# An attention, mixture and gated-layer kernel: its opening written out as one list of single steps

## The chip, the cores and the metric

The kernel runs on one core of one Trainium2 chip. The metric is the device time of one execution in microseconds (us). Of the engines, TensorE (PE) multiplies, its weight load (PEld) runs beside it, VectorE (DVE), ScalarE (ACT) and GpSimd (POOL) do the elementwise work, and SyncE (SP) issues nearly all transfers. Each engine runs its own instructions in the order in which the program lists them.

## The reference

```
# q, k, v: (4, 8, 576, 64) f32; chunks of 64 along the sequence
scores = q_c @ k_c.T / sqrt(64);  attn = softmax(scores);  out = attn @ v_c
x = out laid out as (2304, 512)
p = domain_probs / (sum + 1e-9)
x1 = sum_e p[:, e] * (relu(x @ w1[e]) @ w2[e])        # 4 experts, 512 -> 1024 -> 512
y  = (silu(x1 @ w_gate) * (x1 @ w_val)) @ w_out        # 512 -> 1536 -> 512
```

## The kernel before, in words

Tokens go in 18 blocks of 128; a pass holds 6 blocks (two halves of 3), and there are three passes for each of the two layers. Products are made in float16 from a high and a low part of each operand (three products for one). A weight set n is a 512 x 256 part of w1, loaded as four quarters of 128 x 1024 numbers in all. From set 3 on, a set is multiplied by a seven-product scheme on sums and differences of quarters (`PRODUCTS`, `product`, tiles `lx`, `lz`, `lw`); sets 0 to 2 of the first pass are made plainly, as 12 plain products (`plain`, tiles `plx`, `ply`, `plz`, `plw`) of 12 matmuls of 128x384 each.

The first pass starts while the attention of its own six blocks is still being made. For a block a: `att_scores` (s), `att_max`, `att_sub`, `att_exp` (e), `att_parts` and `att_sums` (row sums, hs, sm, rs), `att_turn` and `att_turned` (transpose et), `att_values` (av), `att_scale`, `att_out` (transpose xt), then `out_high`, `out_copy` and `out_low`, which write the float16 high and low parts (b11, b21 for blocks 0 to 2; t4, b22 for blocks 3 to 5) and a float32 copy x0. `first_sums`, `first_sum4` and `first_split` make t1 to t4 from these copies.

Before float16 parts are made, values and weights are scaled by a power of two that comes from a norm. For the values v of each block and for each w1 set this norm is a sum of squares on ScalarE (`squares`, tile waste), summed over partitions by a one-column product with ones on TensorE (`total`). The scaling of w1 (`w1_scaled`, L548) and of w2 (`w2_scaled`, L837) is a multiply on GpSimd, for all 16 sets, in place, before the sums of quarters (L558, DVE), the high part (ACT, L137) and the low part (POOL, L138).

The order of the opening is a string of one-letter steps, `FIRST_BLOCKS`; after it come a few hand-placed groups (`next_plain`, `ahead`) up to the first seven-product step, and then a loop over products with work put off by `later` (a count of products) and `next_of_rest` (the attention of blocks 6 to 17). PSUM places are named A, X, Y (two buffers each), Z and W (one each). In the opening a load of q, k or v for a later block is issued where the place that it takes is read for the last time.

Of the kernel before, what the change touches and what calls it, by code (L numbers as in the profile page):

```python
# [95 lines left out]
def attention_moe_gated(  # L96
# [251 lines left out]
    def att_scores(a, where):  # L348
        s = att[a]
        ps = att_ps(f"s{a}", where)  # L350
        for i in range(NPAIR):
            for c in range(2):
                b = slice(64 * c, 64 * c + 64)
                nc.tensor.matmul(
                    ps[b, 2 * i : 2 * i + 2], s["q"][:, i, b], s["k"][:, :, i, c], start=True, stop=True
                )
        if next_in_place(a) is not None and a not in (4, 5):
            att_load(next_in_place(a))
        s["s"] = ps
        if a >= BLOCKS:  # L360
            att_max(a)
            att_sub(a)
# [43 lines left out]
    def att_parts(a):  # L406
        s = att[a]
        w = CH // 2
        whole = s["hs"] = by_pair(st_p.tile([P, H, w], F32, tag="hs", name=f"hs{a}", bufs=1))
        part = pairs(s["e"])  # L410
        nc.gpsimd.tensor_tensor(out=whole, in0=part[:, :, :, :w], in1=part[:, :, :, w:], op=ALU.add)
        part = whole[:, :, :, : w // 2]
        nc.gpsimd.tensor_tensor(out=part, in0=part, in1=whole[:, :, :, w // 2 :], op=ALU.add)

    def att_sums(a):
        s = att[a]
        sm = st_p.tile([P, H], F32, tag="sm", name=f"sm{a}")
        part = s["hs"][:, :, :, : CH // 4] if a < HALF else pairs(s["e"])
# [17 lines left out]
    def att_values(a, where):  # L436
        s = att[a]
        ps = att_ps(f"av{a}", where)
        for i in range(NPAIR):
            for c in range(2):  # L440

                nc.tensor.matmul(
                    ps[64 * c : 64 * c + 64, 2 * i : 2 * i + 2],
                    s["et"][:, 2 * i + c, :], s["v"][:, :, i, c], start=True, stop=True,
                )
        if next_in_place(a) is not None and a not in (4, 5):
            att_load_v(next_in_place(a))
        s["av"] = ps
        if a >= BLOCKS:
            att_scale(a)  # L450
# [42 lines left out]
    def out_low(a):  # L493
        for i, (h, l) in enumerate(out_ops(a)):
            r = slice(2 * i, 2 * i + 2)
            if a % HALF == HALF - 1:
# [6 lines left out]
    def first_sums(j):  # L503


        b1, b2 = x_first[0, j], x_first[1, j]
        d0, d1 = slice(0, 2), slice(2, 4)
        sub(b1[:, d0], b2[:, d0], b1[:, d0])
        sub(b2[:, d0], b2[:, d1], b2[:, d0])
        sub(b2[:, d1], b2[:, d1], b1[:, d0])  # L510

    def first_sum4(j):
        b1, b2 = x_first[0, j], x_first[1, j]
# [1 line left out]

    FIRST_PLACES = {"t1": (0, slice(0, 2)), "t3": (1, slice(0, 2)), "t2": (1, slice(2, 4)), "t4": (0, slice(2, 4))}

    def first_split(b, j):
        half, d = FIRST_PLACES[b]
        r = slice(j * P, (j + 1) * P)  # L520
        h, l = x_slots(0, b)
        split(h[:, :, r], l[:, :, r], x_first[half, j][:, d], nc.gpsimd if b in ("t3", "t4") else None)


    raw1, wop = {}, {}
# [598 lines left out]
    with tc.manual_schedule():  # L1124
# [51 lines left out]
        att_load(2)  # L1176
        nc.scalar.activation(junk, ident[:, :1], AF.Exp)
        att_load_v(1)
        att_load(3)
        att_load_v(2)  # L1180
# [11 lines left out]

        def plain_done():
            done(*made_plain.pop(0))

        def next_plain():
            plain_product(plain_banks[12 - len(pieces)])
            plain_done()

        def tick():  # L1200
            for f in deferred.pop(now[0], []):
# [17 lines left out]
        def own_col(n):  # L1219
            cols[n] = small(f"col_{n}", 1, BF16)  # L1220
            squares(raw1[n][:, 0:4].rearrange("p b f -> p (b f)"), cols[n], f"w1_{n}")

        def own_scale(n, place):
            w1_scale_of(n, total(cols[n], f"w1_{n}", places[place]))

        def own_col2():
            cols["w2"] = w2_col(0, BF16)

        def own_scale2(place):
            w2_scale_of(0, total(cols["w2"], "w2", places[place]))  # L1230

        cols = {}

# [9 lines left out]
        stages = {  # L1243
            "s": at(att_scores), "m": at(att_max), "d": at(att_sub), "x": at(att_exp), "p": at(att_parts),
            "r": at(att_sums), "t": at(att_turn), "c": at(att_turned), "v": at(att_values), "u": at(att_scale),
            "o": at(att_out), "h": at(out_high), "y": at(out_copy), "l": at(out_low),
            "f": lambda n: fetch_w1(n, False), "F": fetch_w1, "k": att_load_v, "L": att_load,
            "n": att_norm, "N": lambda a, b, place: att_norms(a, b, places[place]),
            "a": own_col, "b": own_scale, "A": lambda i: w2_greatest(0, i), "B": lambda i: own_col2(), "C": lambda place: own_scale2(place),
            "D": lambda i: w2_scaled(0, i), "S": w1_scaled,  # L1250
            "w": lambda i: w_plain(i // 2, HALVES[i % 2]),
            "P": lambda place: plain_product(place.lower()), "E": plain_done, "G": second_weights, "g": lambda j: split_w2(0, j), "q": lambda i: shares(),
        }
        FIRST_BLOCKS = (
# [4 lines left out]
        )  # L1259
        for step in FIRST_BLOCKS.split():  # L1260
            stages[step[0]](*(int(c) if c.isdigit() else c for c in step[1:]))
        del raw1[0], raw1[1], raw1[2]
        now[0] = -10
        fetch_w1(4)
        fetch_w1(5)
        next_plain()
        first_sums(0)
        tick()
        next_plain()
        first_sums(1)  # L1270
        split_w2(0, 2)
        tick()
        next_plain()
        first_sums(2)
        split_w2(0, 3)
        tick()
        next_plain()
        for j in range(HALF):
            first_split("t2", j)
        for _ in range(3):  # L1280
            tick()

        rest = []
        for a in range(BLOCKS, NS + 2):
# [44 lines left out]


        two = layer2(0)

        def ahead(*makes):

            if len(rest) % 2 == 0:
                next_plain()
            for _ in range(9):
                next(two)
            for make in makes:
                make()  # L1340
            next_of_rest()
            tick()

        def first_t3():
            for j in range(HALF):
                first_split("t3", j)

        def first_t1():
            for j in range(HALF):
                first_split("t1", j)  # L1350

        def first_sum4s():
            for j in range(HALF):
                first_sum4(j)

        ahead(first_t1, lambda: w_sums(raw1[3], None, 0), lambda: make_w(3, 0), lambda: fetch_w2(1, 0), lambda: fetch_w2(1, 1))
        ahead(first_sum4s, lambda: make_w(3, 2), lambda: fetch_w2(1, 2), lambda: fetch_w2(1, 3))
        ahead(lambda: w_sums(raw1[3], None, 1), first_t3, lambda: w2_scale_later(1, 1, 0))
        ahead(lambda: make_w(3, 4))
        for j in range(HALF):  # L1360
            later(1 + j, lambda j=j: first_split("t4", j))
        for j in range(4):
            later(4 + j, lambda j=j: split_w2(1, j))

# [171 lines left out]
```

## Time and profile before

| what | us |
|---|---|
| median of 3 runs (lowest, highest) | 1228.3 (1227.84, 1230.06) |
| the profiled execution, its span | 1228.85, 1227.0 |
| PE busy, share of the span | 1164.1 (95%) |
| DVE busy | 899.2 (73%) |
| ACT busy | 617.5 (50%) |
| POOL busy | 611.0 (50%) |

A share over the whole span hides stages with different limits: PE's clock row stands at full nearly everywhere except in the first tenth and around a quarter of the span. Durations of PE rows are modelled ends; how far apart the starts of consecutive rows are tells what a matmul costs in a stream.

### The profile page before, as it was taken

What the parts mean: (1) busy time and instruction counts of PE and PEld (TensorE: products, weight loads), DVE (VectorE), ACT (ScalarE), POOL (GpSimd) and SP (SyncE); (2) the same over time, 40 slices, a digit from 0 to 9 for tenths busy, and PEclk for the clock granted to TensorE, in tenths of its full rate; (3) what the DMA queues carried; (4) which work ended last, traced back from release to release, by engine and by line L of the source; (5) the groups of instructions that cost most, each with busy time, mean ns of one, the idle gap of its engine ahead of it and who ended that gap; (6) DMA issues with size and microseconds to landing.
All of it is one profiled execution on the core that took longest, in us unless ns stands there. A gap on an engine that the chain in (4) does not pass through costs nothing.

```text
span 1227.0 us, 20554 instructions
## 1 busy us (share of the span) xinstructions
PE 1164.1 (95%) x7287; PEld 693.4 (57%) x7287; DVE 899.2 (73%) x1738; ACT 617.5 (50%) x1263; POOL 611.0 (50%) x533
## 2 busy tenths in 40 slices
PE   6788999999889999999999999999999999999998
PEld 5445555555445545555555555555666666766766
DVE  6478667676556779897758988666488876787577
ACT  6545656564454445564645455435544444444442
POOL 4338665779874467774637776601143222222121
PEclk9789999999899999999999999999999999999999
DMA  7327456556686464757567765573565554455433
GB/s 240 106 86 244 150 191 206 187 161 203 201 301 187 153 213 171 244 182 265 169 203 246 247 214 193 165 239 103 126 233 180 180 184 152 155 188 189 144 117 104
DMA packets 157528, 227.57 MB, mean 185 GB/s; under 512 B 15201, under 2 KB 77281, under 8 KB 157425
## 3 DMA queue, kind: packets, MB, share of 16 engines
q1 hardware_dynamic: 156496, 224.78, 56.8%
q10 hardware_dynamic: 896, 1.44, 0.4%
q8 instruction: 57, 0.93, 0.3%
q14 instruction: 47, 0.38, 0.1%
q0 software_dynamic: 32, 0.04, 0.0%
HBM read 166.17 MB, written 60.03 MB: 184 GB/s over the span
## 4 chain that ended last, share of the span: by engine, by line
PE 55%; DVE 6%; DMA 4%; POOL 2%; issue 2%; ACT 2%; SPq 1%; POOLq 0%; DVEq 0%; ACTq 0%
PE lx L955 6%; PE lx L956 6%; PE lx L957 6%; PE y L1006 6%; PE y L1008 6%; PE y L1004 6%; PE ox L1073 4%; PE oz L1073 4%; PE lz L955 3%; PE lz L957 3%; PE lz L956 3%; DMA w<-w 2%; PE lw L955 1%; PE lw L956 1%; PE lw L957 1%
## 5 line engine op out<-in xcount | busy, mean ns | idle before, releaser
L1006 PE MATMUL y<-w,hh 128*128 128x512 f16 x576 | 220.0, 382 | 7.6 <-POOL w L138 7.6
L1004 PE MATMUL y<-w,hh 128*128 128x512 f16 x576 | 220.1, 382 | 3.7 <-ACT hh L879 2.0
L138 POOL TENSOR_TENSOR ol<-sg,oh 128x384 f16<-128x384 f32 x72 | 75.1, 1052 | 295.1 <-ACT oh L137 253.2
L1008 PE MATMUL y<-w,hl 128*128 128x512 f16 x576 | 219.9, 382 | 0.8 <-DVE hl L882 0.8
L955 PEld LDWEIGHTS <-w 128*128 128x128 f16 x1182 | 116.5, 99 | 83.6 <-issue 5.5
L956 PEld LDWEIGHTS <-w 128*128 128x128 f16 x1182 | 116.4, 98 | 83.2 <-issue 9.7
L957 PEld LDWEIGHTS <-w 128*128 128x128 f16 x1182 | 116.4, 99 | 82.5 <-issue 7.1
L138 POOL TENSOR_TENSOR w<-raw,w 128x512 f16<-128x512 f32 (+1 forms) x96 | 107.7, 1134 | 78.3 <-ACT w L137 52.0
L879 ACT ACTIVATE hh<-sum_p 128x384 f16<-128x384 f32 x90 | 46.8, 520 | 196.1 <-DVE sum_p L943 195.7
L1102 DVE SCALAR_TENSOR_TENSOR acc<-y,pg,acc 128x512 f32<-128x512 f32 x126 | 92.0, 744 | 67.3 <-PE y L1008 65.3
L1008 PEld LDWEIGHTS <-hl 128*128 128x128 f16 x576 | 56.6, 98 | 79.0 <-issue 10.3
L943 DVE TENSOR_TENSOR sum_p<-lx,p 128x384 f32<-128x384 f32 x81 | 44.8, 553 | 66.6 <-PE lx L957 61.5
L1004 PEld LDWEIGHTS <-hh 128*128 128x128 f16 x576 | 56.7, 98 | 64.5 <-ACT hh L879 2.5
L1006 PEld LDWEIGHTS <-hh 128*128 128x128 f16 x576 | 56.7, 98 | 63.2 <-issue 3.7
L138 POOL TENSOR_TENSOR w_made<-raw,w_made 128x512 f16<-128x512 f32 (+1 forms) x48 | 55.2, 1164 | 33.9 <-ACT w_made L137 31.3
L882 DVE SCALAR_TENSOR_TENSOR hl<-sum_p,hh 128x384 f16<-128x384 f32 x90 | 68.9, 765 | 2.7 <-ACT hh L879 2.3
L137 ACT ACTIVATE w<-raw 128x512 f16<-128x512 f32 (+1 forms) x96 | 55.2, 587 | 28.6 <-POOL raw L548 15.8
L137 ACT ACTIVATE oh<-sg 128x384 f16<-128x384 f32 x72 | 36.1, 521 | 62.6 <-DVE sg L903 62.3
L137 ACT ACTIVATE o<-sg 128x384 f16<-128x384 f32 x54 | 26.7, 518 | 66.0 <-DVE sg L217 66.0
L939 ACT COPY u<-lx 128x384 f32<-128x384 f32 x81 | 38.3, 473 | 40.7 <-PE lx L957 39.6
L955 PE MATMUL lx<-t3h,w 128*128 128x384 f16 x162 | 53.2, 328 | 2.9 <-ACT u L939 2.9
L955 PE MATMUL lx<-t2h,w 128*128 128x384 f16 x162 | 52.8, 326 | 3.3 <-DMA w<-w 2.3
(283 smaller groups left out, 3145.5 us busy)
## 6 DMA issues: line engine op xcount, KB each, us to landing
w<-w SPq DMA_DIRECT2D x339, 256.0 KB, 3.8
w<-w SPq DMA_DIRECT2D x81, 128.0 KB, 3.7
raw<-w SPq DMA_DIRECT2D x19, 512.0 KB, 4.6
w<-w_made SPq DMA_DIRECT2D x36, 256.0 KB, 4.2
wo_t<-wo_t SPq DMA_DIRECT2D x36, 256.0 KB, 3.0
raw<-w SPq DMA_DIRECT2D x32, 256.0 KB, 3.3
sums<-x SPq DMA_DIRECT2D x40, 192.0 KB, 4.0
xt<-sums SPq DMA_DIRECT2D x40, 192.0 KB, 3.2
```

The source lines that it names most:

```text
L137: nc.scalar.activation(h, src, AF.Copy)
L138: (lo or nc.vector).tensor_tensor(out=l, in0=src, in1=h, op=ALU.subtract)
L879: nc.scalar.activation(h, src, AF.Relu)
L882: nc.vector.scalar_tensor_tensor(out=l, in0=src, scalar=0.0, in1=h, op0=ALU.max, op1=ALU.subtract)
L955: nc.tensor.matmul(ps, w[:, 0, c], xh[:, k], start=f, stop=False, skip_group_check=True)
L956: nc.tensor.matmul(ps, w[:, 0, c], xl[:, k], start=False, stop=False, skip_group_check=True)
L957: nc.tensor.matmul(ps, w[:, 1, c], xh[:, k], start=False, stop=e, skip_group_check=True)
L1004: nc.tensor.matmul(y, hh[:, c], w[:, 0], start=(j == 0), stop=False)
L1006: nc.tensor.matmul(y, hh[:, c], w[:, 1], start=False, stop=False)
L1008: nc.tensor.matmul(y, hl[:, c], w[:, 0], start=False, stop=(j == 3))
L1073: nc.tensor.matmul(o, left[:, c], w[:, k, right], start=start and t % 2 == 0 and k == 0 and i == 0, stop=k == 1 and i == 2, skip_group_che ...
L1102: nc.vector.scalar_tensor_tensor(out=sum_, in0=y, scalar=p, in1=sum_, op0=ALU.mult, op1=ALU.add)
```

## The change

The whole opening, up to the first seven-product step, becomes one string of single steps. In it:

- `gram` takes over the norm of the values of blocks 0 to 4 and of w1 sets 0 to 5: eight products of a 128x128 piece (the upper half-words of the float32 numbers, read as bfloat16) with itself, added up in PSUM, then one DVE reduction of 128x128 to a column. Block 5 keeps the squares on ScalarE.
- `w1_scaled` and `w2_scaled` run on ScalarE in place of GpSimd, in the opening and in the rest of the first pass and at the start of the second.
- `att_parts` on GpSimd serves all six blocks; some of `first_sums` and of the low parts in `first_split` go from DVE to GpSimd.
- The scaling of the w2 rows of group 1 and of sets 4 and 5 is in the list, before the first seven-product step.
- Loads of q, k, v for a later block are steps of their own (`L`, `k`).

```diff
-        if next_in_place(a) is not None and a not in (4, 5):
+        if next_in_place(a) is not None and a >= BLOCKS:
             att_load(next_in_place(a))
...
+    def gram(src, col, name, where):
+        pool, tag = where
+        ps = pool.tile([P, 512], F32, tag=tag, name=f"gram_{name}")[:, :P]
+        top = src.bitcast(BF16).rearrange("p (n t) -> p n t", t=2)[:, :, 1]
+        n = src.shape[1] // P
+        for i in range(n):
+            x = top[:, i * P : (i + 1) * P]
+            nc.tensor.matmul(ps, x, x, start=i == 0, stop=i == n - 1)
+        with nc.allow_low_precision("a bound, which is rounded to a power of two"):
+            nc.vector.tensor_reduce(out=col, in_=ps, op=ALU.max, axis=AX.X, apply_absolute_value=True)
...
     def w1_scaled(n, some=slice(0, 4)):
         r = raw1[n][:, some]
-        nc.gpsimd.tensor_scalar(out=r, in0=r, scalar1=w1_scale[weights_of(n)], scalar2=None, op0=ALU.mult)
+        nc.scalar.activation(r, r, AF.Copy, scale=w1_scale[weights_of(n)])
...
     def w2_scaled(G, i):
         r = raw2[G, i].rearrange("p b f -> p (b f)")
-        nc.gpsimd.tensor_scalar(out=r, in0=r, scalar1=w2_cols[G, i], scalar2=None, op0=ALU.mult)
+        nc.scalar.activation(r, r, AF.Copy, scale=w2_cols[G, i])
...
-        next_plain()
-        first_sums(1)
-        split_w2(0, 2)
-        tick()
...
-        ahead(first_sum4s, lambda: make_w(3, 2), lambda: fetch_w2(1, 2), lambda: fetch_w2(1, 3))
...
         FIRST_BLOCKS = (
-            "s0W s1A f0 k3 m0 d0 x0 n0 t0A m1 s2Z d1 c0 p0 x1 N00A m2 r0 n1 v0W d2 t1X s3Y p1 u0 c1 o0A N11A m3 x2 r1 n2 v1X f1 s4Z p2 d3 y0 "
...
+            "k2 L3 s0Z s1W m0 d0 x0 m1 d1 x1 p0 J1Z s2A t0Z c0 t1Y r0 m2 p1 J0W d2 c1 f0 v0A u0 r1 f1 J2X v1Y x2 u1 L4 p2 o0W t2Z "
...
+            "w5 v5Z o3A j3X o4A PW r5 G u5 o5Y A0 A1 k6 B0 y4 h4 h3 h5 b3Y f4 l4 f5 y3 l3 CA PZ S3 D0 M5 E D1 y5 j4X L7 Z0 PX PY q0 "
```

In the string J and j are the products of a block's values and of a w1 set with themselves, P a plain product with its PSUM place, E the high and low parts of its result, S and D (and R for group 1) the scaling of w1 and w2, Z and H `first_sums` on GpSimd and on DVE, U and T `first_split` with the low part on GpSimd and on DVE, Y a number of steps of the second layer's products, X a step of the attention of blocks 6 on.

TensorE, from the first block's scores on, before (s, av: scores and values of a block, et, xt: transposes):

```order
L354 MATMUL s0_280<-kbd0_218,q0_257 64x128 x8
L354 MATMUL s1_293<-kbd1_220,q1_261 64x128 x8
L386 MATMUL et0_317<-ident_63,e0_312 128x128 x4
L354 MATMUL s2_324<-kbd2_222,q2_267 64x128 x8
L213 LDWEIGHTS ones_67
L213 MATMUL total_v0_341<-v_cols_68,ones_67 128x1
L442 MATMUL av0_354<-vbd0_219,et0_335 64x128 x8
```

The same place now:

```order
L354 MATMUL s0_280<-kbd0_218,q0_257 64x128 x8
L354 MATMUL s1_289<-kbd1_220,q1_261 64x128 x8
L432 LDWEIGHTS vbd1_221
L432 MATMUL gram_v1_311<-vbd1_221 128x128
...
L354 MATMUL s2_321<-kbd2_222,q2_267 64x128 x8
L386 MATMUL et0_330<-ident_63,e0_300 128x128 x4
L386 MATMUL et1_337<-ident_63,e1_305 128x128 x4
```

The eight products of block 1's values with themselves stand ahead of block 2's scores and of the first transpose.

GpSimd before, around the low parts t4l and b22l of blocks 3 and 4, which the second half of the plain products reads:

```order
L217 TENSOR_TENSOR t4l_0_697<-x0_3_703,t4h_0_696 128x2x128
L217 TENSOR_TENSOR b22l_0_699<-x0_3_703,b22h_0_698 128x2x128
L837 TENSOR_SCALAR raw2_0_0_644<-raw2_0_0_644,col2_0_0_795 128x1024
L217 TENSOR_TENSOR t4l_0_697<-x0_4_781,t4h_0_696 128x2x128
L217 TENSOR_TENSOR b22l_0_699<-x0_4_781,b22h_0_698 128x2x128
```

The same place now:

```order
L217 TENSOR_TENSOR t4l_0_841<-x0_4_838,t4h_0_840 128x2x128
L217 TENSOR_TENSOR b22l_0_843<-x0_4_838,b22h_0_842 128x2x128
L217 TENSOR_TENSOR t4l_0_841<-x0_3_863,t4h_0_840 128x2x128
L217 TENSOR_TENSOR b22l_0_843<-x0_3_863,b22h_0_842 128x2x128
L217 TENSOR_TENSOR x0_0_468<-x0_3_863,x0_0_468 128x256
```

The scaling of the w2 rows no longer stands between the low parts, and a difference of `first_sums` follows them.

ScalarE before, around the parts of set 5 in the loop over products (hh: high part of a first-layer result, p: copy of a product, sm and et: attention):

```order
L137 ACTIVATE w_5_4_1549<-raw1_5_853 128x512
L879 ACTIVATE hh_2_1_1_1587<-sum_p5_4_1585 128x384
L171 ACTIVATE waste_w2_2_1_1592,col2_2_1_1591<-raw2_2_1_1467 128x1024
L404 COPY et9_1601<-et9_1596 128x512
L171 ACTIVATE waste_v9_1608,v_cols_68<-vbd1_221 128x1024
L879 ACTIVATE hh_2_0_1_1618<-sum_u_4_1616 128x384
```

The same place now:

```order
L137 ACTIVATE w_5_4_1626<-raw1_5_861 128x512
L894 ACTIVATE hh_2_1_1_1664<-sum_p5_4_1662 128x384
L563 ACTIVATE raw1_6_1353<-raw1_6_1353,s1_6_1569 128x512
L171 ACTIVATE waste_w2_2_1_1669,col2_2_1_1668<-raw2_2_1_1544 128x1024
L404 COPY et9_1678<-et9_1673 128x512
L171 ACTIVATE waste_v9_1685,v_cols_68<-vbd1_221 128x1024
L894 ACTIVATE hh_2_0_1_1695<-sum_u_4_1693 128x384
```

The scaling of the next set (L563) now stands in ScalarE's queue between two high parts that TensorE waits for.

## Rows read from the trace of the kernel before

**Rows 1.** Busy time by stretch: PE, PEld, DVE, ACT, POOL; then PE clock, DMA share.

```profile
0.00:92.10 92.10, 69.35 (x518) 44.76 (x518) 54.91 (x140) 50.74 (x105) 35.06 (x46) 0.85 0.44 144
92.10:260.00 167.90, 155.56 (x1094) 93.28 (x1093) 120.68 (x275) 100.74 (x218) 114.54 (x81) 0.99 0.57 186
304.00:322.00 18.00, 11.98 (x47) 5.18 (x46) 6.87 (x14) 6.45 (x14) 13.54 (x11) 0.72 0.71 244
341.00:356.00 15.00, 10.54 (x49) 5.12 (x48) 7.44 (x12) 7.16 (x16) 14.84 (x11) 0.89 0.88 316
360.00:1227.00 867.00, 849.69 (x5223) 510.02 (x5221) 660.95 (x1217) 416.88 (x841) 372.76 (x346) 1.00 0.58 185
```

**Rows 2.** Timeline of TensorE: start, duration, line, instruction, idle before and releaser.

```profile
10.01 1.09 PE L354 MATMUL s<-kbd,q 128*64 128x128 f32 x16
...
11.14 1.09 PE L442 MATMUL av<-vbd,et 128*64 128x128 f32 x16
12.17 0.66 PE L386 MATMUL et<-ident,e 128*128 128x128 f32 x4
...
35.28 0.50 PE L955 MATMUL plx<-b11h,w 128*128 128x384 f16 x1
...
39.45 0.33 PE L955 MATMUL plz<-b11h,w 128*128 128x384 f16 x1
...
41.40 0.60 PE L386 MATMUL xt<-ident,e 128*128 128x128 f32 x4
41.84 0.33 PE L955 MATMUL plx<-b11h,w 128*128 128x384 f16 x1
...
57.18 0.48 PE L956 MATMUL plx<-t4l,w 128*128 128x384 f16 x1 [4.01 <-POOL t4l L217]
...
92.12 0.34 PE L955 MATMUL lx<-b11h,w 128*128 128x384 f16 x1
...
94.55 0.38 PE L1004 MATMUL y<-w,hh 128*128 128x512 f16 x1
...
97.14 0.33 PE L955 MATMUL lx<-t2h,w 128*128 128x384 f16 x1
```

**Rows 3.** Timeline of ScalarE, block 1's values.

```profile
11.59 1.06 ACT L171 ACTIVATE waste_v<-vbd 128x1024 f16<-128x1024 f32 x1 [0.17 <-DMA vbd<-vt]
```

**Rows 4.** Groups of instructions in 0 to 92.1: count, busy us, mean ns, idle.

```profile
L171 ACT ACTIVATE waste_w<-raw 128x1024 f16<-128x1024 f32 x7 | 7.4, 1056 | 0.0
L137 ACT ACTIVATE w<-raw 128x512 f16<-128x512 f32 x7 | 4.3, 622 | 5.4 <-POOL raw L837 3.5 <-DVE raw L558 1.8
L141 ACT ACTIVATE w<-raw,s 128x512 f16<-128x512 f32 x6 | 4.1, 728 | 1.9 <-DVE s L175 1.9
```

**Rows 5.** Scaling on GpSimd, whole span: duration ns min/median/max, first and last start.

```profile
L548 POOL TENSOR_SCALAR raw<-raw,s x28: 1558/1568/3215, 62.8 to 343.1; 128x512 f32<-128x512 f32 x24, 128x1024 f32<-128x1024 f32 x4
L837 POOL TENSOR_SCALAR raw<-raw,col x16: 2835/2850/3404, 53.6 to 333.2; 128x1024 f32<-128x1024 f32 x16
```

**Rows 6.** Timeline of TensorE, 304 to 356.

```profile
308.98 0.61 PE L1004 MATMUL y<-w,hh 128*128 128x512 f16 x1 [2.00 <-ACT hh L879]
312.99 0.59 PE L1006 MATMUL y<-w,hh 128*128 128x512 f16 x1 [3.40 <-POOL w L138]
...
318.60 0.43 PE L956 MATMUL lz<-b22l,w 128*128 128x384 f16 x1
...
349.84 0.59 PE L1006 MATMUL y<-w,hh 128*128 128x512 f16 x1 [3.60 <-POOL w L138]
```

**Rows 7.** Timeline of ScalarE at the longest wait in that place.

```profile
307.92 0.63 ACT L137 ACTIVATE w<-raw 128x512 f16<-128x512 f32 x1 [7.44 <-POOL raw L548]
```

**Rows 8.** Waits of GpSimd, 92 to 360: us, times, longest.

```profile
POOL raw L837 <- DVE col L833: 5.5, 4, 2.5
POOL raw L548 <- DMA raw<-w: 4.5, 1, 4.5
```

**Rows 9.** Sums of w1 quarters on DVE, whole span: duration ns min/median/max.

```profile
L558 DVE TENSOR_TENSOR raw<-raw x64: 411/424/1749, 74.2 to 370.6; 128x256 f32<-128x256 f32 x64
```

More of the change, by code (lines that the diff above doesn't have):

```diff
@@ L408, in att_parts @@
         w = CH // 2
-        whole = s["hs"] = by_pair(st_p.tile([P, H, w], F32, tag="hs", name=f"hs{a}", bufs=1))
+        whole = s["hs"] = by_pair(st_p.tile([P, H, w], F32, tag="hs", name=f"hs{a}", bufs=2))
         part = pairs(s["e"])
@@ L445, in att_values @@
                 )
-        if next_in_place(a) is not None and a not in (4, 5):
+        if next_in_place(a) is not None and a >= BLOCKS:
             att_load_v(next_in_place(a))
@@ L491, in out_copy, with out_low @@
         nc.scalar.activation(t, att[a]["xt"], AF.Copy, scale=sigma[:, a : a + 1])
[L493 removed]
+    def out_low(a, early=False):
         for i, (h, l) in enumerate(out_ops(a)):
             r = slice(2 * i, 2 * i + 2)
[L496 removed]
+            if early:
                 nc.vector.scalar_tensor_tensor(
@@ L521, in first_split @@
         h, l = x_slots(0, b)
-        split(h[:, :, r], l[:, :, r], x_first[half, j][:, d], nc.gpsimd if b in ("t3", "t4") else None)
+        split(h[:, :, r], l[:, :, r], x_first[half, j][:, d], eng)
     raw1, wop = {}, {}
@@ L1221, in own_col, with own_gram, own_col2, own_scale2 @@
             squares(raw1[n][:, 0:4].rearrange("p b f -> p (b f)"), cols[n], f"w1_{n}")
+        def own_gram(n, place):
+            cols[n] = small(f"col_{n}", 1, BF16)
+            gram(raw1[n][:, 0:4].rearrange("p b f -> p (b f)"), cols[n], f"w1_{n}", places[place])
         def own_scale(n, place):
             w1_scale_of(n, total(cols[n], f"w1_{n}", places[place]))
[L1226 to L1230, printed above, removed]
+        def own_col2(G):
+            cols["w2", G] = w2_col(G, BF16)
+        def own_scale2(place, G):
+            w2_scale_of(G, total(cols["w2", G], f"w2_{G}", places[place]))
         cols = {}
@@ L1331, in attention_moe_gated @@
         two = layer2(0)
[L1333 to L1354, printed above, removed]
@@ L1356, in attention_moe_gated @@
-        ahead(first_t1, lambda: w_sums(raw1[3], None, 0), lambda: make_w(3, 0), lambda: fetch_w2(1, 0), lambda: fetch_w2(1, 1))
-        ahead(first_sum4s, lambda: make_w(3, 2), lambda: fetch_w2(1, 2), lambda: fetch_w2(1, 3))
-        ahead(lambda: w_sums(raw1[3], None, 1), first_t3, lambda: w2_scale_later(1, 1, 0))
-        ahead(lambda: make_w(3, 4))
+        stages = {
+            "s": at(att_scores), "m": at(att_max), "d": at(att_sub), "x": at(att_exp), "p": at(att_parts),
+            "r": at(att_sums), "t": at(att_turn), "c": at(att_turned), "v": at(att_values), "u": at(att_scale),
+            "o": at(att_out), "h": at(out_high), "y": at(out_copy), "l": at(out_low),
+            "f": lambda n: fetch_w1(n, False), "k": att_load_v, "L": att_load,
+            "n": att_norm, "N": lambda a, b, place: att_norms(a, b, places[place]),
+            "a": own_col, "j": own_gram, "J": at(att_gram), "M": lambda a: out_low(a, True), "b": own_scale, "A": lambda i: w2_greatest(0, i), "B": lambda i: own_col2(0), "C": lambda place: own_scale2(place, 0),
+            "D": lambda i: w2_scaled(0, i), "S": w1_scaled,
+            "H": first_sums, "Z": lambda j: first_sums(j, nc.gpsimd), "V": first_sum4,
+            "U": lambda b, j: first_split(f"t{b}", j, nc.gpsimd), "T": lambda b, j: first_split(f"t{b}", j, None),
+            "K": lambda half: w_sums(raw1[3], None, half), "Q": lambda i: make_w(3, i),
+            "z": lambda j: fetch_w2(1, j), "e": lambda i: w2_greatest(1, i), "I": lambda i: own_col2(1), "O": lambda place: own_scale2(place, 1),
+            "R": lambda i: w2_scaled(1, i), "Y": lambda k: [next(two) for _ in range(k)], "X": next_of_rest, "i": tick,
+            "w": lambda i: w_plain(i // 2, HALVES[i % 2]),
+            "P": lambda place: plain_product(place.lower()), "E": plain_done, "G": second_weights, "g": lambda j: split_w2(0, j), "q": lambda i: shares(),
+        }
@@ L1360, in attention_moe_gated @@
+        FIRST_BLOCKS = (
[6 rows of a table added]
+        )
+        now[0] = -FIRST_BLOCKS.split().count("i")
+        for step in FIRST_BLOCKS.split():
+            stages[step[0]](*(int(c) if c.isdigit() else c for c in step[1:]))
+        del raw1[0], raw1[1], raw1[2]
         for j in range(HALF):
-            later(1 + j, lambda j=j: first_split("t4", j))
+            later(1 + j, lambda j=j: first_split("t4", j, nc.gpsimd))
         for j in range(4):
```

51 lines of the change are left out of this document (8 added, 43 removed), and 7 rows, old and new, of the table FIRST_BLOCKS.

## The prediction

> **What bounds the kernel now.** I read the table by stretch first [rows 1]. From 360 on TensorE is busy 849.69 of 867 at full clock, and the change alters no instruction there; that stretch is bound by products and stays. Three others are not. In the opening, up to the first seven-product step at 92.12 [rows 2], TensorE is busy 69.35 of 92.1 at a mean granted clock of 0.85, and no other engine is busy for 60% of it: the bound is the order in which results travel between engines. From 304 to 322 and from 341 to 356 TensorE stands still for 6.02 and 4.46, the clock is 0.72 and 0.89, and GpSimd is busy 14.84 of the last 15: there GpSimd is the bound. Between (92 to 260) TensorE idles 12.3 of 167.9 with DVE at 72%, GpSimd at 68% and ScalarE at 60%.
>
> Second I read TensorE's timeline. In the opening [rows 2] the first plain product starts at 35.28, and the second half of them, at 57.18, had waited 4.01 for a low part (t4l) from GpSimd. Around 310 and 350 [rows 6] three waits of 2.00, 3.40 and 3.60 end with a ScalarE high part or a GpSimd low part of w2, and the starts after them stand at twice the usual distance. Third, ScalarE at that place [rows 7]: the high part that TensorE waits for stands behind an instruction that waited 7.44 for the scaling of w1 on GpSimd. So one late engine, GpSimd, is behind all three.
>
> **The change, part A: the opening.** Prices at full clock from distances between starts [rows 2]: values (av) 12.17 - 11.14 = 1.03; scores with a one-column total 11.14 - 10.01 = 1.13, so 1.03 and 0.10; a group of four f32 transposes 41.84 - 41.40 = 0.44; a plain product (12 matmuls) 41.40 - 39.45 = 1.95; twelve second-layer matmuls 97.14 - 94.55 = 2.59. A product of a tile with itself has no row. Its eight pieces each load 128x128 weights and run 128 columns. The nearest row is the transposes, four such pieces in f32 in 0.44, so eight take 0.88. From below, eight one-column totals with their loads are 0.80; from above, the transposes' 0.88 at the low one of the two clock levels, 1.2 GHz, is 1.76. I take 0.88, so 11 of them add 9.7 (8.8 to 19.4) to TensorE. What they replace on ScalarE is mostly 1.056 each [rows 4], off the path except where a norm is awaited. Their 11 reductions on DVE, even at 0.42 (a 256-number sum, [rows 9]), are 4.7 beside 37 of idle DVE in the stretch.
>
> Now TensorE in the new order. The eight products of block 1's values come third in its queue, ahead of block 2's scores and all transposes, and these values land at about 11.59 [rows 3]; in the old order TensorE was already at block 2's scores at 10.01. So it stands until 11.59. If it never waited again:
>
> To the first plain product: 6 norm products (5.28), scores 2 to 5 (4.12), values 0 to 2 (3.09), 7 transpose groups (3.08), 2 totals (0.2): 15.8, so 27.4 against 35.28. To the second half of the plain products: 6 plain products (11.7), 5 transpose groups (2.2), 3 values (3.09), 4 norm products (3.52), 5 totals (0.5): 21.0, so 48.4 against 57.18. To the first seven-product step: 6 plain products (11.7), one norm product, 36 second-layer matmuls (7.77), 3 scores, 1 values, 1 transpose, 3 totals: 25.2, so 73.6 against 92.12.
>
> It will wait somewhere. Where the second half starts, the low parts of block 3 come last in GpSimd's row, behind a ScalarE copy that itself follows six others, and the total for w2 ahead of it needs a PSUM place that this same copy frees. The old wait there was 4.01, partly because a 2.85 scaling [rows 5] stood between the low parts; that scaling is gone from the row, so I allow one wait of 4.0 in all, half-clock losses included: 77.6, a gain of 14.5. The ends: 73.6 (gain 18.5), and the first 15.8 wholly at 1.2 GHz, which adds 15.8: 89.4 (gain 2.7).
>
> **Part B: scaling leaves GpSimd.** There are 24 instructions of 1.568 and 20 wide ones of about 2.85 [rows 5], 94.6 in all, 53 to 343. GpSimd gets back some 12 in the opening (pair sums, low parts, differences), where it is busy 35.06 of 92.1. On ScalarE the scaling has no row; the nearest are the scaled high part, 0.728 against 0.622 unscaled for 512 numbers, and 1.056 for 1024 [rows 4]. So 0.73 for a narrow one and 1.056 + 0.106 = 1.16 for a wide one: 17.5 + 23.2 = 40.7, of which 8.1 (seven wide ones) stands in the opening and 33 behind it.
>
> Around 310 and 350 the three waits go (9.0). The clock loss goes with them: from 312.99 to 318.60 TensorE is busy at half rate, 2.8 lost, and 341 to 356 at a mean of 0.89 loses about 1.2. That is 13.0; with the small waits of the two windows (10.48 idle in all) it is 14.5, the upper end. Late next is ScalarE: for sets 16 to 18 the scaling is queued three products after the load is asked for. GpSimd waited 4.5 there once for the landing [rows 8]; on ScalarE high parts and product copies stand behind such a wait, and TensorE waits for them. I take 2 off: a gain of 11.0. The lower end is 5, with that wait and one of the three old ones left.
>
> **Part C: between, and the rest of the pass.** ScalarE goes from 60% to about 72% (33 over the 267 from 77 to 344), GpSimd from 68% to about 36%. The first makes high parts later, the second frees low parts and the DVE sums that waited for scaled weights. TensorE's 12.3 of idle time bounds what can be won. I take 0, and 5 either way (two fifths of those 12.3).
>
> A row on the price of sharing: the sum of two quarters, 256 numbers, takes 0.424 in the median and up to 1.749 with GpSimd busy beside it [rows 9]. The Trainium skill, page "SBUF — State Buffer", section "Who interferes with whom", says that a DVE instruction with two SBUF inputs and a GpSimd instruction that reads SBUF exclude each other for a whole instruction; this row's spread agrees. By that rule the change cuts both ways: it slows DVE in the opening, where differences and low parts move to GpSimd, and speeds it in the loop. By the sum above the loop gives nothing; by the rule it gives something, which is a rival below.
>
> **The sum.** The profiled execution took 1228.85 (span 1227.0 and 1.85 around it), 0.55 over the median of 1228.3. 1228.85 - 14.5 - 11.0 + 0 = 1203.4; I say 1203.
>
> **The rivals.**
> 1. ScalarE takes GpSimd's place as the late engine around 310 and in the loop: part B gives 5 and part C costs 5. 1228.85 - 14.5 - 5 + 5 = 1214. For it: ScalarE's row is in order and carries every high part; against: it waited 7.44 for GpSimd at the worst place, and that goes.
> 2. The opening keeps its waits: TensorE's early norm products wait for loads, the clock drops, and each later step is late by a little. Half of the floor's gain, 9, less another 3 for a second wait: 6. 1228.85 - 6 - 11 = 1212. For it: the old opening lost over 30 against its own work at full clock; against: first products no longer need ScalarE's squares.
> 3. The exclusion of DVE and GpSimd decides in the loop: with GpSimd half as busy, DVE sums fall to 0.42 and part C gains 5. 1198. For it: the 1.749 in [rows 9]; against: TensorE's idle time there is mostly waits in a chain.
> 4. Slower: ScalarE blocks. About 36 scalings stand behind the opening in its row, each with a wait for a column from DVE or for a landing that GpSimd so far took on itself (5.5 in 4 and 4.5 in 1, [rows 8]). If TensorE pays for each of them, 0.7 each (25.5 in all) eats both gains, and from there on it is slower; at 0.9 each it is 32: 1228.85 - 25.5 + 32 = 1235. Against: five waits in all on GpSimd, and ScalarE runs later in the order than GpSimd did.
> 5. The opening only trades waits (gain 2.7) and part B is paid back by part C: about 1227, no change.
>
> **How the numbers follow.** Forecast 0.53, rivals 1 to 5: 0.15, 0.13, 0.07, 0.07, 0.05. A change under 0.2% can't be told from none here. Faster: forecast and rivals 1 to 3, 0.88; same 0.05; slower 0.07. The forecast's own parts reach from 1228.85 - 18.5 - 14.5 - 5 = 1191 to 1228.85 - 2.7 - 5 + 5 = 1226, but not all ends meet at once; I cut to 1194 and to 1217, which takes in rivals 1 to 3 and leaves 4, 5 and the far ends outside.
>
> **What would show it.** Right: the first plain product near 27 to 30, the first seven-product step near 78, the eight products of a norm in 0.9, no wait of TensorE over 2 on GpSimd between 280 and 350, and GpSimd under 45% busy in that stretch. Wrong: a first plain product after 33; norm products at twice the distance; ScalarE named as what TensorE waits for throughout the loop, with its own waits for landings or columns in front; or a stretch behind the first pass that is longer than 867.

## The result, and the profile after

The changed kernel takes 1189.86 us (median of 4 runs, 1186.89 to 1191.75) against 1228.2: a ratio of 0.9683, interval 0.966 to 0.9706. The direction was as forecast, the size was not: the time lies below the forecast range. The profiled execution is the 1191.75 one, with a span of 1190.0, 37.0 less than before. One run reported below (experiment 11, 1211.72 at a granted clock of 0.949) was slow as a whole, and the ratio given there leaves it out.

I laid the two traces over each other at the start of each set's first product. A set's lead is that start before, minus the same start now.

| set | before | now | lead | won since the row above |
|---|---|---|---|---|
| 3 (first seven-product step) | 92.12 | 72.81 | 19.3 | 19.3 |
| 5 | 128.31 | 107.13 | 21.2 | 1.9 |
| 12 | 266.02 | 240.12 | 25.9 | 4.7 |
| 14 | 295.33 | 269.43 | 25.9 | 0.0 |
| 15 | 319.52 | 284.03 | 35.5 | 9.6 |
| 17 | 355.03 | 315.00 | 40.0 | 4.5 |
| end of the span | 1227.0 | 1190.0 | 37.0 | -3.0 |

The rows for sets 12, 14 and 15 in TensorE's timeline, before (start, duration, line, instruction):

```profile
266.02 0.33 PE L955 MATMUL lx<-b11h,w 128*128 128x384 f16 x1
295.33 0.33 PE L955 MATMUL lx<-b11h,w 128*128 128x384 f16 x1
319.52 0.33 PE L955 MATMUL lx<-b11h,w 128*128 128x384 f16 x1
```

and now:

```profile
240.12 0.33 PE L970 MATMUL lx<-b11h,w 128*128 128x384 f16 x1
269.43 0.33 PE L970 MATMUL lx<-b11h,w 128*128 128x384 f16 x1
284.03 0.33 PE L970 MATMUL lx<-b11h,w 128*128 128x384 f16 x1
```

From 12 to 14 both kernels need 29.3; from 14 to 15 the old one needs 24.2 and the new one 14.6.

Busy time by stretch of the changed kernel, to hold against [rows 1] (length, then PE, PEld, DVE, ACT, POOL, then PE clock and DMA share):

```profile
0.00:72.80 72.80, 64.93 (x602) 46.74 (x603) 54.23 (x141) 45.03 (x86) 36.37 (x57) 0.98 0.58 197
72.80:240.00 167.20, 160.91 (x1123) 95.76 (x1122) 112.62 (x272) 118.54 (x244) 60.50 (x58) 0.99 0.58 186
240.00:340.00 100.00, 98.73 (x540) 52.35 (x539) 68.75 (x128) 71.84 (x143) 58.92 (x49) 1.00 0.79 263
280.00:350.00 70.00, 68.73 (x378) 37.06 (x377) 47.97 (x82) 43.96 (x88) 39.65 (x31) 1.00 0.78 254
340.00:1190.00 850.00, 829.49 (x5110) 498.06 (x5108) 646.77 (x1194) 402.70 (x809) 367.67 (x342) 1.00 0.58 183
```

Three readings. The opening has gone from 69.35 of 92.1 busy at a clock of 0.85 to 64.93 of 72.8 at 0.98: TensorE is now what bounds it (from 10.65 to 72.81 it is busy 58.41 of 62.16). From 240 to 340 TensorE is busy 98.73 of 100 at full clock; the two holes of [rows 6] are gone. GpSimd has lost about half of its load between (114.54 of 167.9 before, 60.50 of 167.2 now), and ScalarE took it up (100.74 before, 118.54 now).

TensorE's timeline in the opening, against [rows 2]:

```profile
10.65 1.01 PE L432 MATMUL gram_v<-vbd 128*128 128x128 bf16 x8 [0.45 <-DMA vbd<-vt]
...
17.66 0.62 PE L432 MATMUL gram_w<-raw 128*128 128x128 bf16 x8
18.12 0.60 PE L386 MATMUL xt<-ident,e 128*128 128x128 f32 x4
...
25.76 1.09 PE L354 MATMUL s<-kbd,q 128*64 128x128 f32 x16 [2.24 <-DMA kbd<-kt]
27.27 0.33 PE L970 MATMUL ply<-b11h,w 128*128 128x384 f16 x1
...
47.15 0.32 PE L970 MATMUL plx<-t4h,w 128*128 128x384 f16 x1
67.27 0.66 PE L386 MATMUL et<-ident,e 128*128 128x128 f32 x4 [1.01 <-ACT e L382]
...
72.81 0.33 PE L970 MATMUL lx<-b11h,w 128*128 128x384 f16 x1
```

The first plain product starts at 27.27 (35.28 before). The second half of them starts at 47.15 with no wait, where 4.01 stood. Eight products of a norm take 18.12 - 17.66 = 0.46 to 0.47 of TensorE in a stream at full clock (0.55 and 0.56 for the two that stand ahead of values, 0.94 for the first one, at a granted clock of 0.50). The only waits over 1, warm-up aside, are one for a load (2.24) and one for an exponential (1.01).

The scaling, which stood on GpSimd in [rows 5], is on ScalarE now (duration min/median/max, first and last start, forms):

```profile
L563 ACT ACTIVATE raw<-raw,s x26: 705/708/1157, 46.2 to 303.3; 128x512 f32<-128x512 f32 x20, 128x1024 f32<-128x1024 f32 x6
L852 ACT ACTIVATE raw<-raw,col x16: 1133/1151/1173, 47.2 to 295.8; 128x1024 f32<-128x1024 f32 x16
```

Its prices are those estimated: 0.71 (0.73 was taken) and 1.15 (1.16). What TensorE waits for from set 3 to 340 (total, times, longest):

```profile
PE s L354 <- DVE s L163: 3.1, 3, 2.0
PE s L354 <- ACT xb L491: 1.1, 2, 0.5
...
PE y L1021 <- POOL w L138: 0.4, 1, 0.4
```

Of waits for a low part of a weight, 0.4 is left. A single wait of 2.0 stands out, for a scale that DVE makes (s).

### The profile page after: what moved, and what is told of

Read it like the earlier page. It is cut to its first block, busy times and chain, and to the rows that moved or that the text cites. A ratio compares the mean times of both kernels' runs of the same rounds, so it can differ in the third digit from the quotient of the medians.

```text
span 1190.0 us, 20723 instructions
## 1 busy us (share of the span) xinstructions
PE 1154.1 (97%) x7370; PEld 692.9 (58%) x7370; DVE 882.4 (74%) x1732; ACT 638.1 (54%) x1279; POOL 523.5 (44%) x506
## 4 chain that ended last, share of the span: by engine, by line
PE 72%; DVE 11%; issue 4%; ACT 4%; DMA 4%; POOL 3%; SPq 1%; DVEq 0%; POOLq 0%; ACTq 0%
PE y L1023 8%; PE y L1019 8%; PE y L1021 8%; PE lx L970 7%; PE lx L972 7%; PE lx L971 7%; PE ox L1088 4%; PE oz L1088 4%; PE lz L970 3%; PE lz L972 3%; PE lz L971 3%; PE lw L970 2%; PE lw L972 2%; PE lw L971 2%; DVE hl L897 2%
## 5 line engine op out<-in xcount | busy, mean ns | idle before, releaser
L958 DVE TENSOR_TENSOR sum_p<-lw,p 128x384 f32<-128x384 f32 x81 | 44.7, 552 | 20.8 <-ACT p L954 15.8
```

The lines of the kernel that those rows point to most:

```text
L958: nc.vector.tensor_tensor(out=t, in0=ps, in1=snap.pop(name), op=ALU.add)
```

## The experiments

My theory after the result: (a) the gain behind set 3 comes from GpSimd, whose row was so full that it finished low parts late, and not from ScalarE being a better place for the scaling; (b) the opening gains from the order of steps and from the norm products together. The rivals: for (a), DVE's sums, which GpSimd's reads hold up; for (b), that the norm products give nothing, or that the scaling decides there too. Leads below are leads over the kernel before, at set 3 / 12 / 17; the changed kernel has 19.3 / 25.9 / 40.0.

**1. The loop's scaling back on GpSimd.**

```diff
-        nc.scalar.activation(r, r, AF.Copy, scale=w1_scale[weights_of(n)])
+        if n < 6:
+            nc.scalar.activation(r, r, AF.Copy, scale=w1_scale[weights_of(n)])
+        else:
+            nc.gpsimd.tensor_scalar(out=r, in0=r, scalar1=w1_scale[weights_of(n)], scalar2=None, op0=ALU.mult)
# and for w2: the same with G < 2
```

> The changed kernel with its opening as it is, and the scaling of w1 from set 6 on and of w2 from group 2 on put back on GpSimd (36 scalings, 20 narrow and 12 wide counting the two of a group as two, 4 wide ones of w1 among them). Theory 1, a late GpSimd makes the loop slow: the 20.7 that the changed kernel wins behind its opening (lead of 19.3 at the first seven-product step, 40.0 at set 17) goes, so about 1210 (1207 to 1213), and TensorE waits again for GpSimd's low parts around 290 and 330. Rival, the opening hands over more finished work (sets 4 and 5 and group 1 are scaled, GpSimd has no backlog) and the loop wins by that: at most 5 is lost, 1190 to 1195.

Measured: 1207.57 (ratio 0.9828, 0.9801 to 0.9855). Leads 19.9 / 21.8 / 24.3: the opening is untouched, and 15.7 of the lead at set 17 is gone. TensorE's stretch from 240 to 340, and its longest wait there:

```profile
240.00:340.00 100.00, 89.32 (x474) 46.13 (x473) 66.31 (x113) 50.00 (x106) 88.48 (x63) 0.97 0.72 239
```

```profile
PE y L1027 <- POOL w L138: 7.6, 3, 3.6
```

GpSimd is busy 88.48 of 100 again, and TensorE waits for low parts again, 3.6 at the longest, as in [rows 6].

**2. The norms of the opening by ScalarE's squares, as before; the new order and the scaling kept.**

```diff
-            "a": own_col, "j": own_gram, "J": at(att_gram), ...
+            "a": own_col, "j": lambda n, place: own_col(n), "J": lambda a, place: att_norm(a), ...
```

> The changed kernel with the same list, but each norm product replaced, at its place in the list, by the squares on ScalarE. Theory, the products are worth having because they keep 1.25 per norm out of ScalarE's row, in which the parts stand that TensorE waits for: ScalarE gets 11 more wide squares (13.7) in the opening, of which most is on the path since ScalarE is busy 45 of 72.8 there; TensorE gets 5.2 less. First seven-product step at 78 to 84 instead of 72.8, total 1195 to 1201. Rival, the order of the list is what counts and squares are hidden: step at 68 to 73, total 1185 to 1190.

Measured: 1185.34 (0.9644, 0.962 to 0.9668), faster than the changed kernel, so the theory that the products are worth having fell. Leads 21.9 / 30.2 / 45.8. The two largest waits of TensorE in this opening, warm-up aside (total, times, longest):

```profile
PE s L354 <- DMA kbd<-kt: 1.8, 2, 0.9
PE av L457 <- ACT et L404: 1.7, 3, 0.8
```

Neither is for a norm: the squares are off the path even in the fast order, and 88 products of TensorE buy nothing.

**3. Each norm product made twice over (the sum then holds each piece twice).**

```diff
-        for i in range(n):
+        for k in range(2 * n):
+            i = k % n
             x = top[:, i * P : (i + 1) * P]
-            nc.tensor.matmul(ps, x, x, start=i == 0, stop=i == n - 1)
+            nc.tensor.matmul(ps, x, x, start=k == 0, stop=k == 2 * n - 1)
```

> The changed kernel with every norm product made twice (16 pieces in place of 8, the bound twice as large). Prices one norm product at its place. If TensorE itself bounds the opening now, 11 x 0.47 = 5.2 is added: 1195. If chains between engines bound it, the pieces fill waits: 0 to 2 added, 1190 to 1192.

Measured: set 3 starts at 76.07, 3.3 later, for 11 x 0.47 = 5.2 more work: some two thirds of it is on the path, between the two expectations. (Five executions with the same opening and single norm products, those of experiments 1, 5, 6 and 12 among them, start set 3 at 71.49 to 72.87; against the earliest it is 4.6.) The time, 1190.33 (0.9676, 0.9649 to 0.9702), can't be told from that of the changed kernel; the leads 16.1 / 24.3 / 38.4 show that half of the loss at set 3 is made up by set 12. Only the leads answer here.

**4. The kernel before, with the two scalings on ScalarE and nothing else.**

```diff
-        nc.gpsimd.tensor_scalar(out=r, in0=r, scalar1=w1_scale[weights_of(n)], scalar2=None, op0=ALU.mult)
+        nc.scalar.activation(r, r, AF.Copy, scale=w1_scale[weights_of(n)])
# and the same for w2
```

> The kernel before with the scaling of w1 and w2 on ScalarE, nothing else changed. Theory 1 (late GpSimd): it wins what the changed kernel wins behind its opening, some 14 around 310 and 350 and 3 to 7 between, and in the opening some 3 where a 2.85 scaling stood ahead of a low part: 1205 to 1214. Rival (ScalarE becomes the late engine without the new list): 1222 to 1232.

Measured: 1205.44 (0.9811, 0.9773 to 0.9849). Leads 3.5 / 9.2 / 23.3: behind set 3 the two lines win 19.8 alone, about what the whole change wins there (20.7). So the gain behind the opening needs neither the new order nor the norm products. Its stretch, the clock at full here too:

```profile
240.00:340.00 100.00, 98.38 (x551) 52.47 (x549) 69.14 (x139) 71.97 (x141) 60.62 (x51) 1.00 0.73 241
```

**5. The changed kernel with idle GpSimd work where the loop's scaling stood: it reads and writes a tile that nobody else uses.**

```diff
+    def busy(scale, times):
+        for _ in range(times):
+            nc.gpsimd.tensor_scalar(out=idle_work, in0=idle_work, scalar1=scale, scalar2=None, op0=ALU.mult)
...
         nc.scalar.activation(r, r, AF.Copy, scale=w1_scale[weights_of(n)])
+        if n >= 6:
+            busy(w1_scale[weights_of(n)], (some.stop - some.start) // 2)
# and after the scaling of w2, for G >= 2: busy(w2_cols[G, i], 2)
```

> The changed kernel; behind each scaling of the loop (w1 from set 6, w2 from group 2) GpSimd also scales a scratch tile of zeros that nobody reads, 512 numbers in a row and as often as the old scaling had (about 1.57 each), so GpSimd is as full as before, reads SBUF as before, but nobody waits for its scaled weights. Theory 1a, GpSimd's backlog alone makes its low parts late: the loop's win falls by what the kernel with the real scaling on GpSimd lost (16) less the part of its waits for scaled weights: 1200 to 1207, with TensorE's waits for low parts back around 290 and 330. Theory 1b, the direct wait of ScalarE and DVE for scaled weights is what cost: 1189 to 1193.

Measured: 1211.3 (0.9865, 0.983 to 0.99), leads 20.5 / 21.7 / 18.7. It is slower than the theory's expectation, and slower even than experiment 1. The idle work (count, busy us and mean ns, idle) and TensorE's wait:

```profile
L124 POOL TENSOR_SCALAR idle_work<-idle_work,s 128x512 f32<-128x512 f32 x26 | 44.7, 1720 | 0.8
L124 POOL TENSOR_SCALAR idle_work<-idle_work,col 128x512 f32<-128x512 f32 x24 | 41.6, 1734 | 4.2 <-DVE col L857 3.1
```

```profile
PE y L1032 <- POOL w L145: 13.5, 3, 5.9
```

Nothing waits for the idle tile, and still TensorE waits 13.5 for low parts. What costs is the place that the work takes in GpSimd's row, not that somebody needs its result.

**6. The same with idle work that only writes.**

```diff
-            nc.gpsimd.tensor_scalar(out=idle_work, in0=idle_work, scalar1=scale, scalar2=None, op0=ALU.mult)
+            for _ in range(3):
+                nc.gpsimd.memset(idle_work, 0.0)
```

> The same with three fillings of the scratch tile (512 zeros each, 0.52 each as the opening's fillings took) in place of each scratch scaling: GpSimd is as full, but only writes. If the exclusion of DVE and GpSimd by reads (DVE's sums take 0.72 in the mean with the scaling on GpSimd, 0.56 without) makes the small loss of some 0.8 per set in sets 5 to 11, this run keeps that part (lead growing by 5 to 7 from set 5 to set 12, as in the changed kernel) and loses only around 290 and 330: 3 to 6 faster than the run with reads. If the backlog makes both, the two runs agree within 2.

Measured: 1209.05 (0.9852, 0.982 to 0.9884), leads 19.3 / 23.6 / 21.2. The idle work and the wait:

```profile
L125 POOL MEMSET idle_work<- 128x512 f32 x150 | 78.7, 524 | 7.0
```

```profile
PE y L1033 <- POOL w L146: 12.9, 3, 6.5
```

The time is 2.3 below that with reads, between the two expectations, and the intervals overlap. The wait for low parts is nearly the same, 12.9 against 13.5, so at sets 14 to 17 the reads do not matter: the full row does. Between sets 5 and 12 they do, to a degree. The changed kernel wins 4.7 there; writes leave 21.1 to 23.6, 2.5 of it; reads leave nothing (22.4 to 21.7). DVE's 64 sums of quarters over the whole span (count, busy us, mean ns, idle): the kernel before,

```profile
L558 DVE TENSOR_TENSOR raw<-raw 128x256 f32<-128x256 f32 x64 | 46.0, 739 | 7.0 <-POOL raw L548 6.5
```

the changed one,

```profile
L573 DVE TENSOR_TENSOR raw<-raw 128x256 f32<-128x256 f32 x64 | 34.4, 557 | 0.5
```

with idle reads,

```profile
L582 DVE TENSOR_TENSOR raw<-raw 128x256 f32<-128x256 f32 x64 | 38.7, 624 | 0.5
```

and with idle writes:

```profile
L583 DVE TENSOR_TENSOR raw<-raw 128x256 f32<-128x256 f32 x64 | 34.9, 566 | 0.6
```

A sum takes 0.557 on average in the changed kernel, 0.566 with idle writes on GpSimd, 0.624 with idle reads, and 0.739 with the scaling itself there. Sorted by what GpSimd ran during each sum, the traces say more. With writes, 18 sums beside nothing take 0.417 on average, 27 beside fillings alone 0.418, and 17 beside GpSimd's own two-input operations 0.916. With reads, 26 sums beside idle scalings alone take 0.511. By the Trainium skill, page "SBUF — State Buffer", section "Who interferes with whom", a DVE instruction with two SBUF inputs contends with a GpSimd instruction that reads SBUF and not with one that only writes it; these means agree.

Between sets 5 and 12 alone, a sum takes 0.667 in the kernel before, 0.575 with reads, 0.535 with writes, and 0.419 in the changed kernel, where none of the 27 has anything on GpSimd beside it. With writes 7 of the 27 run beside a low part of a weight (0.868): the fillings slow no sum themselves, but in the fuller row the low parts, which read, fall beside the sums. So in this stretch the two runs do not set a full row against reads; the full row acts through reads. The split stays rough also because the two kinds of idle work sum to 86.3 and 78.7, and the scaling that they stand for took 79.8 in experiment 1.

**7. The opening's scaling back on GpSimd, the loop's on ScalarE** (the conditions of experiment 1 reversed).

```diff
+        if n >= 6:
             nc.scalar.activation(r, r, AF.Copy, scale=w1_scale[weights_of(n)])
+        else:
+            nc.gpsimd.tensor_scalar(out=r, in0=r, scalar1=w1_scale[weights_of(n)], scalar2=None, op0=ALU.mult)
# and for w2: the same with G >= 2
```

> The changed kernel with the scaling in the opening (w1 sets 3 to 5, w2 groups 0 and 1; seven wide instructions, about 2.85 each) back on GpSimd and the loop's on ScalarE. Theory: the list leaves GpSimd little slack between the low parts and the parts of w2 that the first second-layer products read, so the opening loses 3 to 8: first seven-product step at 76 to 81, total 1193 to 1198. Rival, GpSimd's row has room: 0 to 1 lost, 1190.

Measured: 1197.55 (0.9758, 0.9721 to 0.9795), leads 10.6 / 18.6 / 32.8: set 3 starts 8.7 later, and 7.3 of that lasts to set 17 (the profiled execution is the slowest of its four, 1201.53; the medians differ by 7.7). The new wait of TensorE is for the PSUM place of a plain product, not where I looked for it, and behind it stands a wait of DVE (both: total, times, longest):

```profile
PE plz L976 <- DVE hl L903: 5.7, 1, 5.7
```

```profile
DVE shares_of L477 <- POOL prob L1230: 9.6, 1, 9.6
```

GpSimd's timeline at that time (start, duration, line, instruction):

```profile
47.21 2.85 POOL L566 TENSOR_SCALAR raw<-raw,s 128x1024 f32<-128x1024 f32 x1
50.05 5.65 POOL L858 TENSOR_SCALAR raw<-raw,col 128x1024 f32<-128x1024 f32 x2
...
57.95 0.31 POOL L1230 TENSOR_TENSOR prob<-prob,prob_sum 128x72 f32<-128x72 f32 x1
```

Three scalings, 8.5 in all, and three differences stand ahead of a small product of 0.31, the shares of the experts. DVE waited 9.6 for it, and the low part hl that frees the place stands behind this in DVE's row. With the scaling on ScalarE the same wait of DVE is 0.4.

**8. Experiment 2, with the total of a w1 norm three products later and the scaling that follows it two later.**

```diff
-                later(9 + i, lambda i=i: w1_scaled(n, slice(2 * i, 2 * i + 2)))
-            later(7, lambda: w1_scale_of(n, total_of(...)))
+                later(11 + i, lambda i=i: w1_scaled(n, slice(2 * i, 2 * i + 2)))
+            later(10, lambda: w1_scale_of(n, total_of(...)))
```

> A try for a better kernel: the list with squares in place of norm products (1185.3), and in the loop the total over partitions of a w1 set's norm made three products later and the scaling two later, where no step of the attention follows it directly; there TensorE waited 2.0 once (start of the ninth block's scores) for DVE to free a PSUM place, 3.1 in all. If that wait goes and nothing replaces it: 1181 to 1184. If the scaling, now next to its first use, holds ScalarE or DVE: 1186 to 1195.

Measured: 1182.74 (0.9633, 0.9602 to 0.9663), as expected. Leads 20.0 / 32.1 / 47.7. Its opening was 2.0 slower than that of experiment 2, though the two have the same one; between sets 3 and 12 it wins 12.1 where experiment 2 wins 8.2.

**9. The new order alone: experiment 2 with both scalings on GpSimd.**

```diff
-        nc.scalar.activation(r, r, AF.Copy, scale=w1_scale[weights_of(n)])
+        nc.gpsimd.tensor_scalar(out=r, in0=r, scalar1=w1_scale[weights_of(n)], scalar2=None, op0=ALU.mult)
# and the same for w2
```

> The new list with both other parts undone: norms by squares on ScalarE, all scaling on GpSimd. What is left is the order of the opening with its moves of pair sums and low parts. If the parts add up (the list with products and scaling on ScalarE leads by 19.3 at the first seven-product step, squares add 2.6, scaling on GpSimd in the opening takes 8.7; behind it 4.4 as with the loop's scaling on GpSimd): lead 13 at the step, 17 at set 17, 1211. If order and scaling need each other: a lead under 8 at the step, over 1216.

Measured: 1212.67 (0.9879, 0.9859 to 0.9899), leads 12.9 / 15.8 / 18.7, as expected. Set 3 starts at 79.25, with the wait of experiment 7 in the same place:

```profile
PE plz L970 <- DVE hl L897: 6.3, 1, 6.3
```

and DVE behind the same small product:

```profile
DVE shares_of L477 <- POOL prob L1224: 10.0, 1, 10.0
```

With experiments 2 and 7 the opening comes apart: 12.9 from the order with its moves of pair sums and low parts, about 9 from taking the scaling off GpSimd (8.7 in experiment 7; 21.9 - 12.9 = 9.0 with squares), and -2.6 from the norm products. These are shares in this sequence: in the old order the same scaling gave only 3.5 at set 3 (experiment 4). They are also rough: at set 3, executions with the same opening differ by 1.4 with norm products (19.3 to 20.6, five of them) and by 3.3 with squares (20.0 to 23.2, four).

**10 to 12. On one chip together: experiment 2 again, experiment 8 again, the changed kernel again.**

> The list with squares in place of norm products once more, beside the changed kernel on one chip: 4 to 5 faster than it if the two single sessions (1185.3, 1189.9) hold, under 1 if they were the chip's.

> Squares and later totals once more, beside the kernel without the later totals: 2 to 3 faster than it if the wait that went counts in full.

> The changed kernel as it is, for the two comparisons: 1187 to 1192.

| kernel | us (lowest, highest) | ratio to before | interval |
|---|---|---|---|
| changed (12) | 1189.94 (1188.07, 1190.99) | 0.968 | 0.9664 to 0.9696 |
| with squares (10) | 1184.47 (1183.34, 1186.39) | 0.9641 | 0.9624 to 0.9657 |
| with squares, later totals (11) | 1181.38 (1181.11, 1211.72) | 0.9616 | 0.9601 to 0.9631 |

With the norm products the kernel is 5.5 slower, somewhat more than the 4 to 5 expected. The later totals win another 3.1, just over the 2 to 3 expected. What TensorE waits for behind set 3 in run 10,

```profile
PE s L354 <- DVE s L163: 3.1, 3, 2.0
PE s L354 <- ACT xb L491: 1.1, 2, 0.6
```

and in run 11:

```profile
PE av L457 <- ACT xb L491: 1.3, 2, 0.7
PE s L354 <- ACT xb L491: 1.1, 2, 0.8
```

The wait of 3.1 for the scale is gone. Run 11 beats both kernels: some 47 less than the kernel before (1228.2 x 0.0384), 8.6 less than the changed one beside it.

## Why the prediction was too cautious

**Bounds.** "One late engine, GpSimd, is behind all three" was right behind set 3, and more than the sum made of it: experiments 1, 4 and 5 show it at the two holes. In the opening it was right in part. There the order gives 12.9 with all scaling left on GpSimd, and the scaling gives 3.5 in the old order and about 9 in the new one, where GpSimd's late work reaches TensorE by way of DVE (experiments 7 and 9).

**Part A: forecast 14.5, measured 19.3.** The step that failed is "so eight take 0.88": a norm product measured 0.47 in a stream, and the 11 took 5.9 in place of 9.7, which is 3.8 of the difference of 4.8. I priced the 16-bit products by f32 transposes of the same shape; even my lower bound, 0.80, was too high. The rest of the term held in size. TensorE stood until 10.65, not "until 11.59" (0.9 better). The allowance of 4.0 for waits was met by 2.24 + 1.01 + 0.41 and small ones, 3.75 in all, but not where I put it, so its size is luck: the second half of the plain products starts at 47.15 without a wait (48.4 forecast without any), and the waits that came are for a load and for ScalarE. The first plain product, "27.4", started at 27.27.

I did not ask what the opening would be without the norm products. With their price halved they still lose 2.6 at set 3 in each of two pairs (19.3 against 21.9, and 20.6 against 23.2 in runs 12 and 10; 1.8 between the means of all executions), since once the order is good TensorE itself is the bound there, and what was moved onto it had been hidden on ScalarE (experiments 2, 3, 10). The rest of the 5.5 lies behind set 3, where both kernels run the same instructions; I have not settled it.

**Part B: forecast 11.0, measured 9.6 + 4.5 = 14.1.** The gain is at the places named, and near the upper end of 14.5 (12.6 in run 12). The step "I take 2 off" for a late ScalarE failed: no wait of TensorE over 0.5 from 280 to 350 is left. That is 2 of the 3.1 missed; the other 1.1 can be the small waits that only the upper end counted. The sign "GpSimd under 45% busy in that stretch" was not met either: it is 39.65 of 70, 57%, against 91% before (63.42 of 70), and that was enough.

**Part C: forecast 0, measured 6.6 between sets 3 and 12** (8.2 in run 12). This is the largest miss, and the step that failed is "I take 0". "The first makes high parts later, the second frees low parts and the DVE sums": both happened, but only the second reached TensorE. Between sets 5 and 12 DVE waited 1.3 for ScalarE's copies p before and waits 7.9 now, and TensorE does not pay for it. TensorE's idle time from set 3 to 260 was 12.3 in 167.9, and to 240 it is 6.3 in 167.2. Between sets 5 and 12 its waits for DVE fell from 7.4 to 2.9, nearly all of the 4.7 won there. Two of them before (total, times, longest):

```profile
PE et L386 <- DVE half_bits L163: 2.3, 2, 1.2
PE total_w L213 <- DVE e L376: 2.2, 2, 1.1
```

and the same two now:

```profile
PE total_w L213 <- DVE e L376: 0.7, 2, 0.3
PE et L386 <- DVE half_bits L163: 0.3, 2, 0.2
```

With idle work these waits for DVE are 6.9 (reads) and 5.2 (writes). None of the four traces shows a wait of TensorE or DVE for GpSimd in this stretch, so late low parts and scaled weights are not what cost there: GpSimd's reads beside DVE's sums made DVE late, and experiment 6 shows that a full row alone brings such reads about. Rival 3 named this mechanism, with a gain of 5, and got the better of the forecast here.

**The rest: forecast 0, measured -3.0** after set 17. The change alters no instruction there, and yet "a stretch behind the first pass that is longer than 867", a sign of being wrong, is met by these 3.0. In run 12 of the same kernel the lead at set 17 is 41.5; runs of it differ by up to 4.9 (1186.89 to 1191.75). The traces place most of it. At 413.63 TensorE waits 1.41 for a copy on ScalarE, which stands behind an instruction that waited 1.74 for a load (0.40 before). At the end the last product of TensorE starts 39.1 earlier than before, but the last output transfer lands only 37.1 earlier: one issue on SyncE takes 2.26 there, and 0.45 before. Run 12 shows both again (1.1 and 1.92), run 10 with squares neither. Why the load and the issue are late stays open.

**The sum.** 1228.85 - 19.3 - 14.1 - 6.6 + 3.0 = 1191.85, the profiled execution within 0.1. All three misses had one sign, and I had let only "not all ends meet at once" cut the range: two of the three had one cause, GpSimd, so they were not independent. Two parts even went past their own upper ends, 19.3 over 18.5 and 6.6 over 5.

**The rivals.** Rivals 1 and 4, ScalarE late or blocked, fail: it carries 18 more from set 3 to 240, DVE's waits for it grew, and TensorE's did not (2.3 from set 3 to 260 before, 1.4 from set 3 to 240 now). Rival 2, an opening that keeps its waits, and rival 5 fail at 72.81 for set 3.

**Not tried:** which steps of the new order give its 12.9, and an order with fewer norm products (those of the values alone, say).

## What to carry to other kernels

An engine at 50% over the span can be full for a stretch; there, everything in its row is late, and even work that nobody waits for makes the rest of it late, so ask of each stretch what stands in that row and which other engine has room. When work moves onto the engine that will bound a stretch after the change, price it against the new bound: what it replaces may have been free. And where several terms rest on one cause, let their errors go the same way when the range is drawn.

## What was not expected of the hardware

- Eight 128x128 bf16 products, each with its own weights and with operands that are every second half-word of f32 data, take 0.47 in a stream at full clock. Their weight loads, 0.097 each, leave no trace in the distance between starts: eight alone would be 0.78.

```profile
L432 PEld LDWEIGHTS <-raw x48: 95/97/98, 17.6 to 53.4; 128*128 128x128 bf16 x48
```

- The same scaling takes 1.568 on GpSimd and 0.708 on ScalarE for 512 numbers, 2.85 and 1.151 for 1024 (GpSimd in [rows 5], ScalarE in the rows of the result): per number ScalarE is 2.9 times as fast here ((2.85 - 1.568) / (1.151 - 0.708)).
- The clock went with the waits: before, 0.92 on average from 280 to 350 (0.72 in [rows 1] from 304 to 322, and 0.50 from 312.99 to 318.60, right behind a wait of 3.40), and 1.00 now; with idle work on GpSimd it fell back to 0.93 (reads) and 0.91 (writes) from 240 to 340. So a hole in TensorE's work cost it more than the hole's own length.
